# A new execution order and new buffer places for a fused window-attention and squared-ReLU kernel

## The chip, the core and the metric

The kernel runs on one core of a Trainium2 chip. The metric is the device time of one execution in microseconds (us); the figure is the median of repeated executions. The engines are PE (matrix products), ACT (activations), DVE (vector work), POOL and SP; POOL, SP and ACT also issue DMA transfers, each into a queue of its own that it works through in order.

## The reference

Sliding-window attention over 8 batches, 8 heads, 576 positions and a head width of 64, followed by a two-layer perceptron with a squared ReLU on the 4608 tokens.

```python
B, H, S, D = q.shape                      # 8, 8, 576, 64
scores = scale * np.matmul(q, k.transpose(0, 1, 3, 2))
mask = np.abs(pos[:, None] - pos[None, :]) <= 32
scores = np.where(mask, scores, -1000000000.0)
attn = softmax(scores)
x = np.matmul(attn, v)                    # heads side by side: 4608 x 512
h = x @ w_in                              # 512 x 2048
r = np.maximum(h, 0.0)
out = (r * r) @ w_out                     # 2048 x 512
```

Inputs and output are float32; inside, the kernel works in bfloat16 with float32 sums.

## The kernel before, in words

**Tiling.** The 576 positions of a batch are cut into three pieces of 192 queries, so there are 24 groups G = 0 to 23. POOL loads pieces of q, k and v from memory with a cast to bfloat16 (`load_qk`, L377; `load_v`, L415) into four `raw` buffers and five `v` buffers, and the weights (L431, L436). The first k and q pieces come through SP and ACT instead, uncast (`load_hw`, L391), and are cast on DVE (L394) and ACT (L393).

**Attention of a group.** q and k have to be turned so that the head width lies on partitions. For G below 9 PE does it (`turn_pe`, L463, with an evacuation at L476 or L477); from G = 9 on, a DMA that transposes does it, issued by SP (`turn_dma`, L491, names td<batch><piece><half>; it reads `raw` and writes `kq`). Then come the scores (L531, S<G>), the exponential on ACT (L554), the mask on DVE (L562), the product with v (L590, P<G>A and B), its normalisation on DVE into `xa` and `xb` (L604, L608), and the turning of the result into the ring `xt`: on PE for G below 9, by two transposing DMAs on SP from G = 9 on (`xturn`, L649 from `xa`, named T<G>a; L652 from `xb`, named T<G>b).

**The perceptron.** Tokens from 1536 on go through the first product in blocks of 512 by a fast scheme with 7 products in place of 8 (`mm1s`, L770, names Q<token>.<m><product>). It needs four sums of parts of `xt`, made on DVE (L742, xs0 to xs3 of a block), and the corrections c22 and c12 that DVE adds while it takes the products out of PSUM (L794). Earlier tokens take the plain product (L690). The second product is plain for the first 512 tokens (L835) and takes the 7-product scheme afterwards (`strassen`, L917, names P<block>.<product>), with sums on DVE (L885) and results evacuated on ACT (L670) or DVE (L949). 36 stores of 256 KB go out through ACT (L847) or SP (L848).

**What sets the order.** `record` lists 1480 operations in a fixed sequence, each with an engine, what it reads and writes, and, for some, a second form for another engine (`alt`). A planner that is not in the file has decided the rest, and its decision is the string `ORDER`: first one token for each recorded operation, a letter for the engine (P, A, D, G for POOL, S for SP) and the planner's due time in ns; then one token for each buffer that an operation uses (492 of them), its place in its pool. `apply` gives every operation its engine and place, and sorts all by due time; each engine gets its instructions in that order. Due times are not waited for: an instruction runs when its engine comes to it and the semaphores of what it depends on are there.

```python
for op in self.ops:
    s = next(order)
    op.start = int(s[1:])
    op.eng_ = ("PE", "ACT", "DVE", "POOL", "SP")["PADGS".index(s[0])]
...
self.out = sorted(self.ops, key=lambda o: (o.start, o.i))
```

`fill` then puts idle products of zeros (L299) into the gaps that the due times leave on PE at the start, 39 at least and one for each 56 ns of a gap, until the first operation that uses PSUM bank 7.

Of the kernel before, what the change touches and what calls it, by code (L numbers as in the profile page):

```python
# [2 lines left out]

ALU = mybir.AluOpType
# [52 lines left out]
    ALTB=300,  # L57
)
# [174 lines left out]
class Gen:  # L233
# [7 lines left out]
    def alloc(self):  # L241
# [155 lines left out]

    def vcopy(self, G):
        return G % 3 > 0 and G >= self.cfg["VC"]

    def load_v(self, b, g, key, after=None):
        G, NV = 3 * b + g, self.cfg["NV"]
        vt = self.V[G % NV]
        for j in range(2):
            k0 = 192 * g - 32 + 128 * j
            lo, hi = max(k0, 0), min(k0 + 128, S_)
            if self.vcopy(G) and j == 0:
                lo += 64
                vs, vf = self.V[(G - 1) % NV][64:128, 1, :, 0:64], vt[0:64, 0, :, 0:64]
                self.p.rec("DVE", lambda e, vs=vs, vf=vf: e.tensor_copy(vf, vs), reads=[("v", (G - 1) % NV, 1)], writes=[("vc", G % NV)],  # L410
# [4 lines left out]
            self.p.rec("POOL", lambda e, j=j, lo=lo, hi=hi, k0=k0: e.dma_start(  # L415
                vt[lo - k0:hi - k0, j, :, 0:64], self.v[b, :, lo:hi, :].rearrange("h p d -> p h d")),
                writes=[("v", G % NV, j)], dma=(f"v{G % NV}{j}", G), key=key, dur=500 + 3 * n, move=(n // 2, 13.5),
                name=f"v{b}{g}{j}", after=after, slack=self.cfg["LSLACK"] if b > 1 else 0)
# [27 lines left out]
    def turn_pe(self, t, b, g, key):  # L446
# [5 lines left out]
        pr = 3 * b + g < self.cfg["PR"]  # L452

        def f(e):
            ps = self.bank(v).bitcast(BF16)
            for j in range(4):
                for x in range(2):
# [5 lines left out]
                    mm = e.transpose(ps[:, n * j + h * x:n * j + h * x + h], at, self.ID[0:h, 0:h])  # L463
# [6 lines left out]
        def src():  # L470
            ps = self.bank(v).bitcast(BF16)[:, 0:4 * n]
            return ps.rearrange("p (j x q) -> p j q x", j=4, x=2) if pr else ps.rearrange("p (j q) -> p j q", j=4)

        if pr:
            dst = dst.rearrange("p j (q x) -> p j q x", x=2)
        fa = lambda e: e.activation(dst, src(), ACTF.Copy)  # L476
        fd = lambda e: e.tensor_copy(dst, src())  # L477
        if t == "q":
            self.p.rec("ACT", fa, reads=[v], writes=w, key=key, dur=act(4 * n), name=f"ev{t}{b}{g}",
                       alt=("DVE", dve(4 * n, not pr), fd) if self.cfg["ALT"] else None, bias=0)  # L480
        else:
            self.p.rec("DVE", fd, reads=[v], writes=w, key=key, dur=dve(4 * n, not pr), name=f"ev{t}{b}{g}",
# [84 lines left out]
    def pv(self, G):  # L567
# [10 lines left out]
        for w in range(2):  # L578
# [15 lines left out]
            rd = [("v", G % NV, w), ("vset", G % NV), pt] + ([("vc", G % NV)] if w == 0 and cfg["VC"] < NG else [])  # L594
# [138 lines left out]
    def mm1s(self, t0, key):  # L733
# [5 lines left out]
        b11, b12, b21, b22 = xt[:, 0:2, r:r + 256], xt[:, 0:2, r + 256:r + 512], xt[:, 2:4, r:r + 256], xt[:, 2:4, r + 256:r + 512]  # L739
        for i, a, b, rd in ((0, b12, b11, st[0] + st[1]), (1, b22, xs[0][:], st[1] + [("xs", 0)]),  # L740
                            (2, b22, b12, st[1]), (3, b21, xs[1][:], st[0] + [("xs", 1)])):
            p.rec("DVE", lambda e, o=xs[i][:], a=a, b=b: e.tensor_tensor(o, a, b, ALU.subtract), reads=rd, writes=[("xs", i)],  # L742
                  key=key, dur=dve(512), name=f"xs{i}.{t0}")
        tag = lambda f, h: [("gt", (t0 // 64 + 4 * h + x) % (GRING // 64), d) for x in range(4) for d in f]
        for m in range(4):
# [46 lines left out]
            def fused(src, tg, u, y, kk, nm, hh=hh, add=add):  # L792
                hs = lambda y=y: self.rt(hh)[:, 512 * y:512 * y + 512]
                add.append(p.rec("DVE", lambda e: e.tensor_tensor(hs(), src(), self.oe(u), ALU.add), reads=[tg, u],  # L794
                                 writes=[(hh, y)], key=kk, dur=dve(512, False), name=nm, uses=[v, hh], after=add[0] if y else None))
                if y or not cfg["FP"]:
# [3 lines left out]
                    p.rec("DVE", lambda e: e.tensor_scalar(src2(), src2(), 0.0, None, ALU.max), reads=rd, writes=rd, key=kk, dur=153 + 0.26 * c,  # L800
# [6 lines left out]

            prod(1, ks[0])
# [3 lines left out]
            one(X, xtag, rt, lo, ks[1], f"{t0}.{m}")  # L812
# [5 lines left out]
            fused(Y, ytag, p5, 0, ks[4], f"c22.{t0}.{m}")  # L818
            prod(3, ks[5])
            fused(X, xtag, u2, 1, ks[5], f"c12.{t0}.{m}")  # L820
            prod(4, ks[6])
            one(Y, ytag, rt2, hi, ks[6], f"{t0}.{m}b")
# [43 lines left out]
    def sums_g(self, g, key):  # L866
# [3 lines left out]
        for c in (0, 1, None):  # L870
            whole = c is None
            if whole and not cfg["S34"]:
# [353 lines left out]
```

## Time and profile before

| | |
|---|---|
| median of 3 runs (lowest to highest) | 286.65 us (286.6 to 287.02) |
| the profiled execution: its span | 287.0 us |
| PE busy | 279.1 us, 97% |
| DVE, ACT, POOL busy | 238.0, 215.7, 115.0 us |
| granted PE clock | 0.999 of full speed |
| loads through POOL's queue | 17.93 MB |
| transposes and stores through SP's queue | 15.34 MB |

The profile is of one execution. Its span runs from the first to the last instruction of the program, the wait for the last stores included; it lies 0.35 us above the median and within the highest run. A row of the timeline reads: start in us, duration in us, engine, line of the kernel, operation, what it writes and reads, how many instructions were merged, and in brackets the idle time of the engine before it with what ended it. PEld is PE's weight load, which is a separate row from the product. SPq and ACTq are DMA issues.

### The profile page before, as it was taken

What the parts mean: (1) busy time and instruction counts of PE and PEld (TensorE: products, weight loads), DVE (VectorE), ACT (ScalarE), POOL (GpSimd) and SP (SyncE); (2) the same over time, 40 slices, a digit from 0 to 9 for tenths busy, and PEclk for the clock granted to TensorE, in tenths of its full rate; (3) what the DMA queues carried; (4) which work ended last, traced back from release to release, by engine and by line L of the source; (5) the groups of instructions that cost most, each with busy time, mean ns of one, the idle gap of its engine ahead of it and who ended that gap; (6) DMA issues with size and microseconds to landing.
All of it is one profiled execution on the core that took longest, in us unless ns stands there. A gap on an engine that the chain in (4) does not pass through costs nothing.

```text
span 287.0 us, 7773 instructions
## 1 busy us (share of the span) xinstructions
PE 279.1 (97%) x3137; PEld 234.6 (82%) x3151; DVE 238.0 (83%) x438; ACT 215.7 (75%) x328; POOL 115.0 (40%) x153
## 2 busy tenths in 40 slices
PE   8999999999999999998999999999999999999995
PEld 8879866787756688886898888888888888888884
DVE  4787797989887798996899989998989978898721
ACT  2787666857868787887887889988887688798620
POOL 8999867194498052076235912605000000000000
PEclk9999999999999999999999999999999999999999
DMA  9999999999999999999999996989941612200233
GB/s 143 165 193 185 204 173 156 156 113 152 119 158 175 190 112 147 190 115 163 163 154 134 151 166 144 132 180 118 145 98 46 130 34 61 75 0 2 73 112 110
DMA packets 162915, 37.57 MB, mean 131 GB/s; under 512 B 150080, under 2 KB 162368, under 8 KB 162880
## 3 DMA queue, kind: packets, MB, share of 16 engines
q0 software_dynamic: 113728, 17.93, 87.7%
q1 hardware_dynamic: 44432, 15.34, 29.8%
q10 hardware_dynamic: 4720, 3.80, 5.1%
q8 instruction: 25, 0.41, 0.6%
q14 instruction: 10, 0.08, 0.1%
HBM read 36.70 MB, written 9.44 MB: 161 GB/s over the span
## 4 chain that ended last, share of the span: by engine, by line
PE 78%; DMA 10%; POOL 6%; DVE 2%; issue 2%; ACT 1%; ACTq 0%; DVEq 0%; POOLq 0%
PE ps L917 31%; PE ps L770 24%; PE ps L690 9%; PE ps L835 4%; POOL raw L377 4%; PE ps L590 3%; DMA w<-in_moe_w_in_dram 3%; PE ps L531 3%; DMA kq<-raw 3%; DMA v<-in_v_dram 2%; POOL v L415 2%; DMA xt<-xa 2%; PE ps L463 1%; DVE rt L794 1%; PE ps L630 0%
## 5 line engine op out<-in xcount | busy, mean ns | idle before, releaser
L665 ACT ACTIVATE rt<-ps 128x512 bf16<-128x512 f32 (+2 forms) x81 | 48.4, 606 | 17.6 <-PE ps L690 7.3
L670 ACT ACTIVATE oe<-ps 128x512 f32<-128x512 f32 x72 | 42.0, 595 | 22.2 <-PE ps L917 15.1
L554 ACT ACTIVATE e<-ps 128x1024 bf16<-128x1024 f32 x48 | 48.8, 1022 | 6.8 <-PE ps L531 5.0
L377 POOL DMA_DIRECT2D raw<-in_q_dram x46 | 36.7, 809 | 42.3 <-DMA kq<-raw 39.0
L377 POOL DMA_DIRECT2D raw<-in_k_dram x46 | 36.8, 816 | 27.2 <-DMA kq<-raw 20.8
L917 PE MATMUL ps<-w,gt 128*128 128x256 bf16 x384 | 47.0, 273 | 0.0
L690 PE MATMUL ps<-xt,w 128*128 128x192 bf16 (+2 forms) x379 | 46.4, 271 | 0.6 <-DMA w<-in_moe_w_in_dram 0.2
L415 POOL DMA_DIRECT2D v<-in_v_dram x48 | 38.6, 814 | 12.4 <-ACT v L412 10.0
L917 PEld LDWEIGHTS ps<-w,gt 128*128 128x128 bf16 x384 | 36.6, 98 | 4.9 <-issue 0.2
L770 PE MATMUL ps<-xs,sw 128*128 128x256 bf16 x288 | 39.9, 272 | 0.0
L690 PEld LDWEIGHTS ps<-xt,w 128*128 128x128 bf16 x384 | 32.4, 98 | 8.8 <-ACT v L412 0.3
L659 ACT ACTIVATE gt<-rt 128x512 bf16<-128x512 bf16 (+2 forms) x51 | 38.7, 777 | 0.3
L794 DVE TENSOR_TENSOR rt<-ps,oe 128x512 bf16<-128x512 f32 x48 | 32.9, 688 | 5.1 <-PE ps L770 3.8
L917 PE MATMUL ps<-ts,gt 128*128 128x256 bf16 x256 | 31.9, 273 | 0.0
L562 DVE TENSOR_TENSOR pt<-e,mask 128x2048 bf16<-128x2048 bf16 (+1 forms) x30 | 30.2, 1007 | 1.9 <-ACT e L554 1.4
L917 PE MATMUL ps<-ts,ss 128*128 128x256 bf16 x256 | 31.7, 273 | 0.0
L770 PEld LDWEIGHTS ps<-xs,sw 128*128 128x128 bf16 x288 | 27.4, 98 | 3.3 <-ACT oe L670 0.2
L770 PE MATMUL ps<-xt,w 128*128 128x256 bf16 x192 | 27.2, 273 | 0.2
L917 PEld LDWEIGHTS ps<-ts,ss 128*128 128x128 bf16 x256 | 24.7, 98 | 3.2
L660 DVE TENSOR_TENSOR gt<-rt 128x1024 bf16<-128x1024 bf16 (+2 forms) x49 | 26.4, 557 | 0.8 <-ACT rt L665 0.7
L917 PEld LDWEIGHTS ps<-ts,gt 128*128 128x128 bf16 x256 | 24.5, 98 | 3.2 <-DVE oe L949 0.3
L770 PEld LDWEIGHTS ps<-xt,w 128*128 128x128 bf16 x192 | 18.1, 98 | 3.3 <-ACT ps L809 0.4
(70 smaller groups left out, 405.2 us busy)
## 6 DMA issues: line engine op xcount, KB each, us to landing
out_dram<-oe SPq DMA_DIRECT2D x23, 256.0 KB, 3.5
out_dram<-oe ACTq DMA_DIRECT2D x13, 256.0 KB, 4.4
v<-in_v_dram POOLq DMA_DIRECT2D x16, 128.0 KB, 5.5
w<-in_moe_w_in_dram POOLq DMA_DIRECT2D x4, 512.0 KB, 9.8
w<-in_moe_w_out_dram POOLq DMA_DIRECT2D x4, 512.0 KB, 16.4
raw<-in_q_dram POOLq DMA_DIRECT2D x18, 96.0 KB, 5.3
raw<-in_k_dram POOLq DMA_DIRECT2D x14, 112.0 KB, 5.3
raw<-in_q_dram POOLq DMA_DIRECT2D x14, 112.0 KB, 6.9
```

The costliest lines, as they stand in the source:

```text
L377: self.p.rec("POOL", lambda e, j=j, dst=dst: e.dma_start(dst, s[j]), writes=[self.rtag(t, b, g, j)], dma=(f"{t}{G % self.cfg['NRAW']}{j}", ...
L415: self.p.rec("POOL", lambda e, j=j, lo=lo, hi=hi, k0=k0: e.dma_start(vt[lo - k0:hi - k0, j, :, 0:64], self.v[b, :, lo:hi, :].rearrange("h ...
L554: last = self.p.rec("ACT", lambda e, ef=ef, v=v: e.activation(ef(), self.bank(v, 0, 2), ACTF.Exp, scale=0.125), reads=[v], writes=tags, ke ...
L562: self.p.rec("DVE", lambda e, pf=pf, ef=ef, mb=mb, n=n: e.tensor_tensor(pf(y=0, n=n), ef(y=0, n=n).rearrange("p (w h q) -> p w h q", w=n, ...
L659: alt = ("ACT", act(c), lambda e: e.activation(dst, src(), ACTF.Square)) if self.cfg["ALT"] else None
L660: self.p.rec("DVE", lambda e: e.tensor_tensor(dst, src(), src(), ALU.mult), reads=rd, writes=wr, key=key, dur=dve(c), name=name, alt=alt, ...
L665: return self.p.rec("ACT", lambda e: e.activation(dst(), src(), ACTF.Relu), reads=rd, writes=wr, key=key, dur=act(c), name=name, alt=alt, ...
L670: self.p.rec("ACT", lambda e: e.activation(dst(), src(), ACTF.Copy), reads=rd, writes=wr, key=key, dur=act(c), name=name, alt=alt, bias=se ...
L690: mm = e.matmul(ht[:, n * x:n * x + n], self.W1[:, ft, 128 * d:128 * d + 128], self.XT[:, ft, r:r + n], start=(ft == 0 and x == 0), stop=( ...
L770: mm = e.matmul(bk[:, 256 * x:256 * x + 256], lhs(k, 256 * m + 128 * x), rhs[:, k, :], start=start and x == 0 and k == 0, stop=(k == 1), s ...
L794: add.append(p.rec("DVE", lambda e: e.tensor_tensor(hs(), src(), self.oe(u), ALU.add), reads=[tg, u], writes=[(hh, y)], key=kk, dur=dve(51 ...
L917: mm = e.matmul(op[:, 256 * y:256 * y + 256], lhs[:, l0[0] + k, a:a + 128], rhs[:, r0 + k, c0:c0 + 256], start=start and y == 0 and k == 0 ...
```

## The change

The configuration gets ten new switches, all off or at the value that leaves the code as it was (`AS=0, PS=0, VS=99, VD=0, ZP=0, XM=0, WIDE=(), JT=0, JM=0, SH=1`), with code behind them that is not reached (`vsplit`, `swapped`, `joint`, `wide`, `pair` and branches in `load_v`, `turn_pe`, `mm1s`, `strassen` and `sums_g`). One allocation is reached:

```diff
-            self.XS = [sb(f"xs{i}", [128, 2, 256], BF16) for i in range(4)]
+            self.XSA = sb("xs", [128, 4, 2, 256], BF16)
+            self.XS = [self.XSA[:, (0, 2, 1, 3)[i], :, :] for i in range(4)]
```

The four buffers become four parts of one, of the same size. What is left of the change is the string `ORDER`: the same number of tokens, with nearly all due times and many places new.

```diff
 ORDER = """
-D900 G1350 A1170 D2200 D5546 D9773 D10213 D10698 D7178 D9553 D11762 D7058 D7598 D10413 D11962 D9453 D5746 D17653 D5256
...
+D850 G2426 A1120 D3076 D3596 D5351 D6811 D10525 D2876 D6491 D9773 D5571 D11477 D4016 D6711 D3496 D1340 D18725 D4301
...
```

Counted token by token, 76 operations go from one of ACT and DVE to the other, 38 each way; 10 stores go from ACT to SP and 3 from SP to ACT, the last one of the program among the 10; no other operation changes its engine. Due times of the operations that the prediction speaks of, in ns (an operation's token is found by its place in the recorded sequence):

| operation | token | before | after |
|---|---|---|---|
| the iota that masks and identity need (POOL) | 2 | G1350 | G2426 |
| q001, the first load on POOL | 39 | G1700 | G850 |
| w11, second quarter of w_in (POOL) | 56 | G11936 | G11436 |
| turnk00, the first product that is not idle | 66 | P7128 | P7681 |
| A0.4, which needs w11 | 157 | P20637 | P20878 |
| T10b, then xs0.1536, which needs it | 526, 547 | S95574, D103850 | S96462, D100990 |
| td500, turning q and k of a later group (SP) | 824 | S110507 | S126368 |
| T13a, then xs0.2048, which needs it | 705, 707 | S122484, D130056 | S122088, D128824 |
| Q1536.33, Q1536.34 (PE) | 616, 620 | P131000, P131650 | P130303, P131614 |
| T15b, then xs2.2560, which needs it | 856, 881 | S149029, D156037 | S148009, D155940 |
| P8.4b, the last product | 1478 | P281083 | P280760 |
| the last store | 1480 | A282859 | S282535 |

On SP's queue the order around T13a becomes:

```
before: T10b T9b T10a td410 st6 td420 td500 T12a td421 T11b td501 T12b T11a T13a td510 td521
after:  T10a T10b td410 td411 td421 st2 td420 T11a T11b st6 st4 T12a T12b T13a td501 td521 st5 td500
```

POOL's 149 instructions keep their kind and number. By due time, 25 of its loads stand between 68 and 90 us (20 before), 20 between 101 and 117 us (7 before), 2 between 117 and 136 us (13 before), 22 between 136 and 154 us (10 before) and 10 from 154 us on (25 before). The idle products that `fill` makes from the due times become 159 in place of 149, and 78 of them stand ahead of turnk00 in place of 68.

More of the change, by code (lines that the diff above doesn't have):

```diff
@@ L57 @@
     ALTB=300,
+    AS=0,
+    PS=0,
+    VS=99,
+    VD=0,
+    ZP=0,
+    XM=0,
+    WIDE=(),
+    JT=0,
+    JM=0,
+    SH=1,
 )
@@ L452, in turn_pe @@
         pr = 3 * b + g < self.cfg["PR"]
+        il = pr and not self.cfg["PS"]
         def f(e):
@@ L811, in mm1s @@
             prod(2, ks[1])
[L812 removed]
+            if cfg["ZP"]:
+                pair(za, 0, X, xtag, None, ks[1], f"{t0}.{m}", ha)
+            else:
+                one(X, xtag, rt, lo, ks[1], f"{t0}.{m}")
             prod(6, ks[2])
@@ L871, in sums_g @@
             whole = c is None
-            if whole and not cfg["S34"]:
+            if whole and not cfg["S34"] or not whole and not cfg["SH"]:
                 continue
@@ L894, in wash @@
         if v.wash:
-            e.matmul(self.bank(v, 1), self.ZZ[:, 0:128], self.ZZ[:, 0:512], start=True, stop=True)
+            for i in range(v.n // 2, v.n):
+                e.matmul(self.bank(v, i), self.ZZ[:, 0:128], self.ZZ[:, 0:512], start=True, stop=True)
     def product(self, g, i, key, v):
```

414 lines of the change are left out of this document (293 added, 121 removed), and 10 rows, old and new, of the table ORDER.

## The prediction

> **What bounds the kernel now.** I read the page first, then the busy time by stages.
>
> ```profile
> span 287.0 us, 7773 instructions
> PE 279.1 (97%) x3137; PEld 234.6 (82%) x3151; DVE 238.0 (83%) x438; ACT 215.7 (75%) x328; POOL 115.0 (40%) x153
> ```
>
> ```profile
> core 0: us, PE busy (x) PEld busy (x) DVE busy (x) ACT busy (x) POOL busy (x), PEclk, DMA share, GB/s
> 1.00:21.00 20.00, 19.31 (x310) 17.39 (x311) 14.09 (x46) 12.52 (x18) 19.68 (x27) 1.00 1.69 174
> 21.00:126.00 105.00, 103.72 (x1200) 81.36 (x1213) 90.83 (x166) 79.89 (x115) 60.41 (x79) 1.00 1.72 157
> 126.00:134.00 8.00, 6.67 (x70) 5.30 (x69) 5.80 (x13) 5.48 (x9) 7.74 (x10) 1.00 2.20 154
> 134.00:283.62 149.62, 149.38 (x1562) 130.52 (x1562) 127.16 (x216) 116.90 (x187) 26.85 (x35) 1.00 0.81 106
> ```
>
> PE is the bound, and its real work is the same in both orders, so the change can only move PE's idle time, the idle products of the start, and the tail. PE is idle 1.28 us in the 105 us to 126, 0.24 us in the last 150 us, and 1.33 us in the 8 us between. That one spot is the largest thing an order could win. The timelines of DVE and of PE's weight loads show what happens there.
>
> ```profile
> 130.02 0.69 DVE L949 TENSOR_TENSOR oe<-ps,oe 128x512 f32<-128x512 f32 x1 [0.74 <-PE ps L917]
> 132.17 0.76 DVE L742 TENSOR_TENSOR xs<-xt 128x512 bf16<-128x512 bf16 x2 [1.46 <-DMA xt<-xa]
> 132.85 0.68 DVE L794 TENSOR_TENSOR rt<-ps,oe 128x512 bf16<-128x512 f32 x1
> 131.55 0.42 PEld L770 LDWEIGHTS ps<-xt,sw 128*128 128x128 bf16 x4
> 133.59 0.33 PEld L770 LDWEIGHTS ps<-xs,w 128*128 128x128 bf16 x4 [1.61 <-DVE rt L794]
> ```
>
> DVE stands 1.46 us in front of xs0.2048, which needs the transpose T13a. Queued behind it is the correction c22.1536.3 (L794, 132.85), and PE's Q1536.34 waits for that one before it may write the bank (133.59). The SP queue tells why the transpose was late.
>
> ```profile
> 116.05 1.22 SPq L491 DMA_TRANSPOSE kq<-raw  x1
> 117.32 1.24 SPq L649 DMA_TRANSPOSE xt<-xa  x1
> 118.66 1.23 SPq L491 DMA_TRANSPOSE kq<-raw  x1
> 119.93 2.19 SPq L652 DMA_TRANSPOSE xt<-xb  x1
> 122.23 1.24 SPq L491 DMA_TRANSPOSE kq<-raw  x1
> 123.51 1.27 SPq L652 DMA_TRANSPOSE xt<-xb  x1
> 124.83 2.58 SPq L649 DMA_TRANSPOSE xt<-xa  x2
> ```
>
> ```profile
> SPq L210 <- DMA raw<-in_q_dram: 11.4, 2, 6.0
> ```
>
> From 116.05 to 127.41 SP issues eight transposes without a pause, most of them 1.2 to 1.3 us. The first, td500, is due at 110.5 in the order and starts 5.5 us late, since SP waits in its queue for a load of q. T13a is the last of the eight: issued by about 126.1 (124.83 plus half of 2.58) against a due 122.5, and read by DVE at 132.17.
>
> ```profile
> 20.99 0.82 PE L690 MATMUL ps<-xt,w 128*128 128x192 bf16 x8 [0.17 <-DMA w<-in_moe_w_in_dram]
> 281.61 1.74 PEld L917 LDWEIGHTS ps<-ts,gt 128*128 128x128 bf16 x16
> ```
>
> The due times may be used as a ruler, not as a price, because PE follows them. A0.4 is due 20.64 and Q1536.33 131.00; they ran at 20.99 (first row here) and 131.55, lags of 0.35 and 0.55. Behind the stall Q1536.34 (due 131.65, ran 133.59) lags 1.94, and P8.4a (due 280.21, the second row) 1.40. So nothing behind the stall makes it good.
>
> **The change part by part.**
>
> *The stall at 132.* In the new SP order td500, td501 and td521 stand behind T13a, td421 stands far ahead, and T11a, T11b, T12a and T12b are spread over 15 us by due time. No load that can be late holds the queue just ahead of T13a. What its landing takes is bounded by the view of its line, min/median/max in the last row.
>
> ```profile
> L649 SPq DMA_TRANSPOSE xt<-xa x15: 1171/1242/2589, 92.8 to 238.6; - x15
> ...
> DMA to landing us min/median/max: 2.3/3.3/7.1
> ```
>
> By due times 6.74 us lie between its issue and its reader (122.09 to 128.82), double the median and 0.4 short of the worst; and only 2 loads are due from 117 to 136, so I take the median. The wait goes. What comes late next on DVE there is nothing: c22.2 (L949) moves behind xs0 and xs1, and its 0.74 us of waiting for PE is then covered. Worth: 1.33 us by PE's idle time, 1.61 by the weight load's; I take 1.33, since products drain while the weight load stands. At the worst landing, 7.1 us, 0.4 us of the wait come back.
>
> *The start.* PE stands on idle products until real work begins, and the fill is made from due times.
>
> ```profile
> 1.19 6.36 PE L299 MATMUL ps<-zz 128*128 128x128 bf16 x68 [1.19 <-DVE zz L293]
> 7.74 0.59 PEld L299 LDWEIGHTS ps<-zz 128*128 128x128 bf16 x10
> 0.83 0.23 POOL L307 IOTA dif<- 128x128 f32 x1 [0.39 <-POOLq L1211]
> 1.39 1.68 POOL L377 DMA_DIRECT2D raw<-in_q_dram  x2 [0.32 <-issue]
> ```
>
> Ten more idle products ahead of turnk00 cost 10 x 0.059 = 0.6 us there. Against that, the iota no longer stands in front of the first load, which starts 1.39 - 0.83 = 0.56 us earlier, and with it the whole queue of loads in front of w11, whose landing ended PE's last wait of the start (0.17 us ahead of A0.4). Between the two lie gaps that are filled with idle products, so most of the 0.6 is absorbed before 21 us. Bounds: -0.2 (w11's wait goes, the rest is absorbed) to +0.6 (all ten carried through). I take +0.1, nearer to the wait's row than to the fill's, as the wait is on the path and the fill is padding.
>
> *The swaps of engine.* Where a form has both engines in the trace:
>
> ```profile
> L670 ACT ACTIVATE oe<-ps 128x512 f32<-128x512 f32 x72 | 42.0, 595 | 22.2 <-PE ps L917 15.1 <-PE ps L770 4.8 <-PE ps L835 0.9
> L669 DVE COPY oe<-ps 128x512 f32<-128x512 f32 x12 | 8.3, 689 | 2.6 <-PE ps L770 1.3 <-PE ps L917 1.2
> L659 ACT ACTIVATE gt<-rt 128x512 bf16<-128x512 bf16 x30 | 18.3, 627 | 0.2
> L660 DVE TENSOR_TENSOR gt<-rt 128x512 bf16<-128x512 bf16 x18 | 7.2, 417 | 0.0
> 284.34 0.38 ACTq L847 DMA_DIRECT2D out_dram<-oe  x1
> ```
>
> 38 go each way, so the sums hardly move: an evacuation is 0.09 us dearer on DVE, a square 0.21 cheaper. ACT loses 7 stores net, 7 x 0.38 = 2.7 us, to SP. All of it lies under PE, which waits 0.24 us in the last 150 us with these engines 85% and 78% busy; cost 0. If that cover were gone, one swap in front of PE is worth about 0.1 to 0.2 us either way.
>
> *The remaining small waits of PE*, 1.28 us before 126 and 0.24 behind 134, belong to other pairs of neighbours in the new order. I take no change, 0.3 either way.
>
> *The tail.* The last store goes from ACT, whose issue took 0.38 us (the row above), to SP, behind a semaphore. No row shows that pair on SP; I bound it by 0 and by one such issue more, 0.4, and take 0, since it is one issue for one issue. Buffer places and the one xs allocation change no instruction: 0.
>
> *Loads in bursts.* This is what the change adds. Loads stand closer: 25, 20 and 22 in three stretches of some 20 us. The transposes run beside them, and the views of lines L652 and L491 give what that does.
>
> ```profile
> L652 SPq DMA_TRANSPOSE xt<-xb x15: 1190/1218/2193, 99.2 to 235.1; - x15
> ...
> DMA to landing us min/median/max: 2.4/4.0/6.5
> L491 SPq DMA_TRANSPOSE kq<-raw x30: 1203/1254/3492, 65.6 to 210.9; - x30
> ...
> DMA to landing us min/median/max: 2.7/4.4/7.9
> ```
>
> Two readers on DVE have a transpose close ahead: xs0.1536 behind T10b (96.46 to 100.99, 4.5 us, six transposes back to back) and xs2.2560 behind T15b (148.01 to 155.94, 7.9 us, inside the burst of 22). At the medians neither waits. At the worst, T10b's reader stands 6.5 - 4.5 = 2.0 us and T15b's 0. By due times no load is issued from 89.1 to 101.2, so I take the median for T10b: 0, with 2.0 kept for the range.
>
> The Trainium skill, "DMA: Bandwidth & Descriptors", section "Issuing engines are not separate DMA queues", speaks against the change here: transfers issued from SP and from POOL end on the same 16 engines and interleave, so a second queue gives no second road. The trace agrees in part: a transpose of one line took 2.7 us at best and 7.9 at worst. By the rule alone the bursts would slow the transposes, and the time would be that of the first or the third rival below.
>
> *Sum:* 287.0 - 1.33 + 0.1 = 285.8 for a profiled span; taken from the median, 286.65 - 1.23 = **285.4 us**. The profiled span lies 0.35 above the median, as one run in three did.
>
> **The rivals.**
>
> *The wait moves.* T10b lands 6.5 us after issue and DVE stands 2.0 us at xs0.1536; the correction c22.1 and PE's P1.4 are queued behind it. PE lost 1.33 of DVE's 1.46 in the old stall, so it loses about 1.9 here, less some 0.5 for the small waits that it has before 126 anyway: 286.65 - 1.23 + 1.4 = 286.8. For it: six transposes in a row, 1.25 us each. Against it: no load is due while the six are issued, and half of this line's transposes landed within 4.0.
>
> *It does not do what it says.* Due times are not waited for; POOL's early loads wait for their raw buffers, and SP for the loads, so the queues could run as before and T13a be late again: 286.65 or up to 0.3 less. Against it: the order in SP's queue itself has changed.
>
> *Slower, by the burst at 136 to 154.* Loads there are twice as dense (22 for 10). If what crowding adds to a transpose, 7.9 - 4.4 = 3.5 us, doubles, T15b lands 4.4 + 7.0 = 11.4 us after issue and DVE stands 3.5 us at xs2.2560, with c22.3 behind it and P3.4 waiting on that. By due times P3.4 stands 0.3 behind c22.3, so PE loses about 3.2: 286.65 - 1.23 + 3.2 = 288.6. It decides from a landing 10.0 us after issue (7.9, the 0.3, the gain of 1.23 and 0.57 more). For it: DMA share 2.20 in the crowded stretch of the table above. Against: no transpose took over 7.9.
>
> **How the numbers follow.** A measurement of this kernel can tell about 0.2%, 0.57 us, from no change. The forecast has 0.64, with its own range 284.8 (the start 0.2 shorter, 1.33 regained, 0.3 of small waits less: 286.65 - 1.83) to 286.0. The moved wait has 0.16 and the change that does nothing 0.06, both near 286.7; the burst has 0.14, from 287 up, as smaller overruns count to it. The range 284.9 to 287.0 leaves out most of the burst and a little at the low end. Faster by over 0.2% 0.64, within 0.22, slower 0.14.
>
> **What would show it.** Right: no DVE wait on xt over 0.3 us near 129, PE idle under 0.5 us between 126 and 134, SP's queue without a run of eight transposes ahead of T13a, A0.4 within 0.4 us of 21. Wrong: a DVE wait on xt near 101 or 156 with PE idle behind it; transposes of L652 over 8 us; A0.4 past 21.5; a second half in which PE idles more than 0.6 us.

## The result and the profile after

The kernel after takes **289.27 us** (median of 4 runs, 288.95 to 292.35) against 286.83 us (4 runs, 286.6 to 287.41): a ratio of 1.0101, 95% interval 1.0068 to 1.0134. Forecast were 285.4 us and a range up to 287.0. Eleven more runs of the same kernel, beside 34 of before, gave a median of 288.74 us (286.61 to 292.89) against 286.88 (286.4 to 288.29), ratio 1.0042 (1.0011 to 1.0072). The ratios leave out executions more than 1.5% above the fastest of their kernel, the medians do not, and with this kernel the difference matters.

The page of after, then its busy time by stages:

```profile
span 287.6 us, 7804 instructions
PE 279.8 (97%) x3161; PEld 236.0 (82%) x3161; DVE 237.1 (82%) x438; ACT 215.9 (75%) x328; POOL 114.7 (40%) x153
```

```profile
core 0: us, PE busy (x) PEld busy (x) DVE busy (x) ACT busy (x) POOL busy (x), PEclk, DMA share, GB/s
1.00:21.00 20.00, 19.16 (x309) 17.59 (x311) 14.52 (x47) 10.22 (x14) 19.62 (x27) 1.00 1.65 175
21.00:126.00 105.00, 104.06 (x1220) 81.64 (x1220) 89.52 (x164) 84.90 (x121) 69.44 (x90) 1.00 1.88 162
126.00:134.00 8.00, 6.22 (x68) 5.13 (x66) 5.34 (x10) 5.61 (x9) 0.82 (x1) 1.00 1.62 189
134.00:285.04 151.04, 150.31 (x1572) 131.67 (x1570) 127.53 (x220) 114.87 (x186) 24.61 (x32) 1.00 0.77 101
```

PE's work is the same, and its last product ends at 284.35, so that 0.69 us of the last row lie behind it. The hole is again between 126 and 134 us, 1.78 us now, but something else makes it. DVE's timeline of after, then PE's weight loads and SP's issues:

```profile
129.62 0.42 DVE L780 TENSOR_TENSOR xs<-xt 128x512 bf16<-128x512 bf16 x1 [0.24 <-PE ps L812]
130.08 0.42 DVE L780 TENSOR_TENSOR xs<-xt,xs 128x512 bf16<-128x512 bf16 x1
132.83 0.69 DVE L1139 TENSOR_TENSOR oe<-ps,oe 128x512 f32<-128x512 f32 x1 [2.32 <-DMA out_dram<-oe]
```

```profile
133.57 0.77 PEld L1107 LDWEIGHTS ps<-ts,gt 128*128 128x128 bf16 x8 [2.05 <-DVE oe L1139]
```

```profile
122.75 1.17 SPq L681 DMA_TRANSPOSE xt<-xa  x1
124.09 2.68 SPq L523 DMA_TRANSPOSE kq<-raw  x2
126.82 0.61 SPq L1036 DMA_DIRECT2D out_dram<-oe  x1
```

The wait for T13a is short in this execution: xs0.2048 runs at 129.62 after 0.24 us of waiting (before: 132.17 after 1.46). T13a landed at 129.44, 6.69 us after its issue, just in front of its reader. The add behind it, c22.2 (L1139), is what stands now. It writes an `oe` buffer, and its releaser is a *store* that still reads that buffer. The store is st5. Before, ACT issued it (due 112.55) and c22.2 had another place; now c22.2 has the place of st5's buffer, and st5 is due at 125.918 on SP, issued at 126.82 behind T13a and two more transposes, and landed 5.89 us later. PE's next products wait 2.05 us for c22.2.

What transposes took from issue to landing, in the views of their lines in after (L681 was L649, L684 was L652, L523 was L491):

```profile
L681 SPq DMA_TRANSPOSE xt<-xa x15: 1171/1190/3100, 90.1 to 233.7; - x15
...
DMA to landing us min/median/max: 2.3/4.6/10.8
L684 SPq DMA_TRANSPOSE xt<-xb x15: 1188/1245/1854, 95.6 to 235.8; - x15
...
DMA to landing us min/median/max: 2.5/4.2/8.9
L523 SPq DMA_TRANSPOSE kq<-raw x30: 1204/1274/2467, 60.6 to 187.7; - x30
...
DMA to landing us min/median/max: 2.7/5.3/9.9
```

At best they are as quick as before (2.3 to 2.7 us); the median of L649's line rises from 3.3 to 4.6 and its maximum from 7.1 to 10.8.

### The profile page after: what moved, and what is told of

Its sections match the earlier page's. It is cut to its first block, busy times and chain, and to the rows that moved or that the text cites. A ratio compares the mean times of both kernels' runs of the same rounds, so it can differ in the third digit from the quotient of the medians.

```text
span 287.6 us, 7804 instructions
## 1 busy us (share of the span) xinstructions
PE 279.8 (97%) x3161; PEld 236.0 (82%) x3161; DVE 237.1 (82%) x438; ACT 215.9 (75%) x328; POOL 114.7 (40%) x153
## 4 chain that ended last, share of the span: by engine, by line
PE 90%; DMA 4%; POOL 2%; DVE 2%; issue 1%; ACT 0%; POOLq 0%; DVEq 0%; ACTq 0%
PE ps L1107 34%; PE ps L812 25%; PE ps L722 15%; PE ps L1023 5%; PE ps L622 4%; PE ps L563 4%; POOL raw L389 2%; DMA out_dram<-oe 2%; DMA v<-in_v_dram 2%; PE ps L495 1%; PE ps L668 1%; PE ps L662 1%; DVE oe L1139 0%; PE ps L311 0%; DVE xa L640 0%
## 5 line engine op out<-in xcount | busy, mean ns | idle before, releaser
L702 ACT ACTIVATE oe<-ps 128x512 f32<-128x512 f32 x75 | 43.8, 595 | 19.4 <-PE ps L1107 14.0
L389 POOL DMA_DIRECT2D raw<-in_k_dram x46 | 36.1, 791 | 22.2 <-DMA kq<-raw 13.2
L691 ACT ACTIVATE gt<-rt 128x512 bf16<-128x512 bf16 (+2 forms) x51 | 40.2, 802 | 0.7 <-DVE rt L847 0.2
L812 PE MATMUL ps<-xs,sw 128*128 128x256 bf16 x288 | 39.2, 273 | 0.1
L692 DVE TENSOR_TENSOR gt<-rt 128x512 bf16<-128x512 bf16 (+2 forms) x49 | 25.7, 544 | 0.8 <-ACT rt L697 0.5
```

Of the source, the lines that this page charges most:

```text
L389: self.p.rec("POOL", lambda e, j=j, dst=dst: e.dma_start(dst, s[j]), writes=[self.rtag(t, b, g, j)], dma=(f"{t}{G % self.cfg['NRAW']}{j}", ...
L691: alt = ("ACT", act(c), lambda e: e.activation(dst, src(), ACTF.Square)) if self.cfg["ALT"] else None
L692: self.p.rec("DVE", lambda e: e.tensor_tensor(dst, src(), src(), ALU.mult), reads=rd, writes=wr, key=key, dur=dve(c), name=name, alt=alt, ...
L702: self.p.rec("ACT", lambda e: e.activation(dst(), src(), ACTF.Copy), reads=rd, writes=wr, key=key, dur=act(c), name=name, alt=alt, bias=se ...
L812: mm = e.matmul(bk[:, 256 * x:256 * x + 256], lhs(k, 256 * m + 128 * x), rhs[:, k, :], start=start and x == 0 and k == 0, stop=(k == 1), s ...
```

## The experiments

Four theories stood against each other. **First:** the late store and the place of c22.2's buffer. **Second:** the crowd of transfers, wherever it falls. **Third:** the start. **Fourth**, formed when a trace of a long execution was there: the order on DVE at 101 us. All kernels but two, in which loads are thinned, are edits of tokens in `ORDER`; a token is an engine letter and a due time, or a buffer's place. Kernels named together shared a chip and its runs of before.

### The stall that the forecast wanted to remove

**The kernel before, once more**, and **the kernel before with td500 moved** away from the front of SP's run of eight transposes:

```diff
-td500: S110507
+td500: S122600
```

Expected of the first:

> The kernel before, profiled once more, with nothing changed. If the wait of DVE on T13a near 132 us belongs to the kernel, this profile shows it again (1.3 to 1.6 us of PE idle between 126 and 134) and its time is that of the runs shown. If it belongs to one execution only, PE is idle under 0.4 us there, the span is about 285.5, and 1.3 us of the predicted gain never were to be had. It also shows how far the time lies above the span.

Expected of the second:

> The kernel before, with one token changed: the transpose td500 goes behind T13a in SP's queue (due 122.6 in place of 110.5), which is the one part of the new order that the prediction's gain rested on. By the prediction T13a is issued near 122.5, the wait of DVE near 132 goes, and the time falls by 1.0 to 1.4 us. If that wait does not stand in the usual executions of before, the time stays within 0.3 us.

Measured: 287.25 us, ratio 1.0008 (0.9991 to 1.0025), and 286.86 us, ratio 1.0009 (0.9993 to 1.0025). The stage from 126 to 134 us of the first:

```profile
126.00:134.00 8.00, 8.00 (x84) 6.69 (x83) 7.26 (x16) 6.72 (x12) 4.27 (x6) 1.00 2.18 172
```

PE never stops there, and it never stops there in the second kernel either (8.00 of 8). Five traces have SP's order ahead of T13a as it is in before, and two of them show the stall: the one that was shown before the prediction, and that of a kernel further down in which v000 comes late. Its row on DVE:

```profile
133.18 0.76 DVE L742 TENSOR_TENSOR xs<-xt 128x512 bf16<-128x512 bf16 x2 [1.36 <-DMA xt<-xa]
```

In these two SP issued td500 at 116.05 and 116.36, in the other three at 111.0 to 111.9. The kernel before, once more:

```profile
111.89 2.69 SPq L491 DMA_TRANSPOSE kq<-raw  x1
```

So the late td500 is there in some executions, and not in the usual one. The execution shown before the prediction was a long one: wherever a span and a run time stand side by side, the time is 1.8 to 2.2 us above the span (289.54 beside 287.6 in after, 287.36 beside 285.5 here), and 1.8 to 1.9 with the kernel before. Its span of 287.0 thus stands for about 288.8 us by this estimate (its own run time is not known), and 4 of 148 executions of before took that long. Nearly nothing of the gain was there to be had in the median.

### The late store

**The kernel after with store 5 early on ACT**, on two chips, and **with store 5 on ACT at its late time**:

```diff
-st5: S125918
+st5: A112650        (early, both chips)
+st5: A125918        (ACT, late)
```

Expected, early:

> The kernel after, with one token changed: the store st5 (result c12.1) is issued by ACT at its place of before (due 112.65) and not by SP at 125.92. Theory of the late store: c22.2 on DVE waits for the place in the oe pool that st5 still holds, so this wait (2.32 us on DVE, 2.05 on PE at 133.6) goes and the time falls by 1.7 to 2.1 us. Rival, crowded DMA queues: transposes and stores around 120 to 134 take 6 to 11 us whatever the store does, the next late one (T13a landed 0.2 us before its reader) takes the wait over, and the time falls by under 0.8 us.

Expected, early, beside the unaltered kernel after:

> The kernel after with store 5 alone issued by ACT at its former due time 112.65 (was SP, 125.918), beside the unaltered kernel after on the same chip. First theory (the late store holds the buffer that the add for group 2 needs): 0.6 to 1.0 % below the kernel after, that is within 0.4 % of the kernel before, and PE busy for all of 126 to 134 us. Second theory (the crowded DMA engines slow transposes and stores in many places): at most 0.3 % below the kernel after, and PE idle elsewhere between 95 and 160 us.

Expected of that unaltered kernel:

> The kernel after, unaltered, once more and on the same chip as the other three. Both theories: 0.7 to 1.3 % over the kernel before (288.8 to 290.6 us). If the late store (first theory) is what takes the time, the profiled execution shows PE idle for 1 to 2.5 us between 126 and 134 us again, with the vector add that writes the oe buffer waiting for a store's transfer; if that stall is absent in this execution, its time should be under 288 us.

Expected, ACT, late:

> The kernel after, with only the engine of st5 changed: ACT issues it, at the same due time of 125.92. If its landing is late because it stands behind the transposes in SP's queue, it lands within 4.4 us (median of ACT's stores before) of an issue near 126.5, c22.2 waits under 0.6 us, and the time falls by 1.4 us or more. If all 16 DMA engines are crowded whatever queue it is, it lands 5.5 to 6 us after issue again and the time falls by under 0.5 us.

Measured: early, 287.57 us, ratio 1.002 (0.999 to 1.005), and on the other chip 286.99 us, 1.0016 (0.9997 to 1.0034), where the unaltered kernel took 288.74 us, 1.0042. That is 0.26% by the ratios, less than the 0.6 to 1.0 that the first theory wanted, and their intervals overlap. The traced execution of the unaltered kernel there (287.61 us) lost only 0.4 us of PE in the stage, with the store landing 3.5 us after its issue. On ACT but late, 287.31 us, 1.0005 (0.9971 to 1.0038). With the store early the stage is full; the kernel of the second chip:

```profile
126.00:134.00 8.00, 8.00 (x86) 6.86 (x84) 7.17 (x14) 7.11 (x11) 1.01 (x1) 1.00 1.72 172
```

On ACT at the late time, the traced execution (span 287.2) still had PE busy 6.50 of these 8 us and DVE waiting 1.67 us for the store. ACT had issued it at 124.44, ahead of its due time and with no transpose in its queue, and it took 7.8 us to land:

```profile
out_dram<-oe ACTq DMA_DIRECT2D x1, 256.0 KB, 7.8
```

That execution was long (289.35 us), and the median and its wide interval do not show such a loss. How much of the hold is the place behind the transposes, and how much the flight of the store, the runs do not tell.

**The kernel before with this cost put in**: store 5 late on SP, c22.2 in its buffer, four other adds moved to make room.

```diff
-st5: A112550   c22.2/st11: place 4
+st5: S125918   c22.2/st11: place 2   (c22.1536.2: 2 to 1, c12.1536.3: 2 to 4, c22.2048.0 and .1: 2 to 4)
```

> The kernel before with the suspected cost put in and nothing else of the change: store 5 goes to SP with the due time 125.918 (was ACT, 112.55), and the add for group 2 (due 129.37) gets the buffer that this store holds; four other adds exchange buffers to make that room. First theory: the add waits until the store has landed (issued at 125.9 to 127, 3 to 6 us in flight, so 129 to 133 us) and the kernel is 0.2 to 1.0 % slower than before, with PE idle 0.5 to 2.5 us between 126 and 136 us. If the buffer and the queue of one store are worth nothing: within 0.2 % of before.

Measured: 287.66 us, ratio 1.0032 (1.0017 to 1.0048). DVE's row and PE's wait:

```profile
130.00 0.69 DVE L949 TENSOR_TENSOR oe<-ps,oe 128x512 f32<-128x512 f32 x1 [1.36 <-DMA out_dram<-oe]
```

```profile
PE ps L917 <- DVE oe L949: 0.7, 1, 0.7
```

In this execution the store was issued at 124.59, even ahead of its due time, and released its buffer at 130.00. The first theory holds: put in, the hold costs 0.32%, clear of noise, and taken out of after it gives back 0.26% of the ratio. It is not all, for the spread of after remained open.

### The crowd, first try

**The kernel after with eight loads thinned**: v511, v500, q600, q511, k601, k511, k600 and q601 (issued 110 to 117 us) move one head of eight.

```diff
+            src = s[j]
+            if f"{t}{b}{g}{j}" in THIN:
+                dst, src = dst[:, 0:1], src[:, 0:1]
```

> The kernel after, in which the eight last loads of the burst of 20 (v511, v500, q600, q511, k601, k511, k600, q601, issued from 110 to 117 us) move one head of eight only, so an eighth of their bytes; their other heads are left out of what is computed with. Store 5 stays on SP behind the transposes. Second theory (crowding): transposes and store 5 around 120 to 130 us land in 3 to 4.5 us instead of 6 to 7, and the time falls by 0.5 to 1.0 %, to within 0.4 % of before. First theory (the place in the queue): the store is still issued at 126 to 127 us and lands 3 to 4 us later, at 130 to 131, so 0.5 to 1.2 us of the wait of 2 to 2.8 stay and 0.4 to 0.8 % over before remain.

Measured: 286.87 us, ratio 0.9991 (0.9972 to 1.001). The store was issued at 127.67, later than in after, but T13a landed after 2.31 us (after: 6.69) and the store after 3.73 (after: 5.89), and PE was busy for all of 126 to 134. So the second theory has a share too: the hold bites because transfers around it are slow. At 5.89 us of flight this store would have landed at 133.56, 2 us behind the 131.52 at which c22.2 ran.

### The start

**v000 back ahead of k021, k020 and v010** in after; the same with store 5 early; and **v000 behind v010 in before**:

```diff
-v000: G8100   (after)        -v000: G7168   (before)
+v000: G5920                  +v000: G8710
```

Expected, after with v000 early:

> The kernel after with one load of the start, v000, back ahead of k021, k020 and v010 on POOL (due 5.92 instead of 8.10), where before had it nearer to; store 5 stays late. Third theory (the start: P0A, due 13.35, waits up to 1.2 us for v000, which lands at 12.7 to 13.9): the wait of the first values product for its load goes, PE is busy at least 19.5 of 20 us from 1 to 21, the time falls by 0.3 to 0.5 %, and the executions over 290.5 us (5 of 11 in the unaltered kernel after, at a mean granted clock of 0.988 to 0.994) become 0 or 1 of 12. First theory (store 5): ratio to before 1.003 to 1.011 as for after, and over 290.5 us in 2 to 5 of 12.

Expected, with store 5 early too:

> The kernel after with v000 early and store 5 early on ACT, both. First theory alone: as with store 5 early alone, ratio 1.001 to 1.003. Third theory added: 0.996 to 1.001, and no execution over 290.5 us (3 of 22 with store 5 early alone).

Expected, before with v000 late:

> The kernel before with v000 put behind v010 on POOL (due 8.71 instead of 7.17), its place in the kernel after. Third theory: P0A (due 12.45) waits 0.5 to 1.5 us for v000 (landing 13 to 13.7 instead of 11.9), and 0.1 to 0.5 % is lost, with executions over 290 us if the start is what makes them. First theory says nothing of it; if the wait at the start is made up for by idle time that the start has anyway (PE has gaps of 5 us in the plan's first 21 us): within 0.1 % of before.

Measured: 288.96 us, 1.0047 (1.0015 to 1.0079), nothing gained; with store 5 early 288.24 us, 1.0028 (0.9998 to 1.0058). In before the late v000 cost 0.72% (0.48 to 0.95): its traced execution shows PE waiting 0.9 us for v000, 0.6 us for a turned k or q, and 1.2 us behind T13a, in the stall of before (its row stands above). The 0.72%, 2.1 us, is more than the wait for v000; how often the other two waits come with it is left open. Four of its nine executions had a mean granted clock of 0.994, which none of 148 of before had, so a late start can bring on such executions. But it is not what brings them on in after, where they stay with v000 early (5 of 12): there the third theory falls.

The first of these kernels gave the trace that was missing, of an execution of 292.4 us. Its busy time by stages:

```profile
95.00:104.39 9.39, 9.23 (x104) 6.93 (x101) 4.72 (x8) 6.83 (x8) 3.14 (x4) 1.00 1.56 166
104.39:107.80 3.41, 0.97 (x13) 0.55 (x11) 2.82 (x7) 1.35 (x2) 1.58 (x3) 1.00 1.77 167
107.80:114.60 6.80, 5.53 (x37) 3.75 (x38) 5.45 (x8) 2.26 (x4) 6.80 (x10) 0.50 2.04 220
114.60:126.00 11.40, 11.40 (x118) 10.26 (x117) 9.26 (x17) 9.56 (x16) 3.96 (x5) 1.00 2.06 155
```

This is one execution, and among the longest. PE does 0.97 us of work in 3.41, and then its granted clock is 0.50 for 6.8 us: a product of 128x256 takes 419 ns in the mean there, and 273 in the unaltered kernel after. The groups of that stretch, and of 95 to 126 us in the unaltered kernel:

```profile
L1107 PE MATMUL ps<-ts,gt 128*128 128x256 bf16 x16 | 3.6, 419 | 1.5 <-DVE oe L1139 1.5
```

```profile
L1107 PE MATMUL ps<-ts,gt 128*128 128x256 bf16 x32 | 3.8, 273 | 1.1 <-DVE oe L1139 1.1
```

The timelines of DVE, ACT and PE's weight loads tell what stopped PE:

```profile
103.89 0.76 DVE L780 TENSOR_TENSOR xs<-xt 128x512 bf16<-128x512 bf16 x2 [4.45 <-DMA xt<-xb]
104.57 0.42 DVE L780 TENSOR_TENSOR xs<-xt,xs 128x512 bf16<-128x512 bf16 x1
105.02 0.21 DVE L636 RECIPROCAL rs<-ps 64x8 f32<-64x8 f32 x1
105.26 0.43 DVE L780 TENSOR_TENSOR xs<-xt,xs 128x512 bf16<-128x512 bf16 x1
105.72 0.69 DVE L640 TENSOR_TENSOR xa<-ps,rs 64x512 bf16<-64x512 f32 x1
```

```profile
106.45 0.60 ACT L646 ACTIVATE ps<-zz 64x520 f32<-64x520 bf16 x1 [3.42 <-DVE xa L640]
```

```profile
107.10 0.31 PEld L622 LDWEIGHTS ps<-v,pt 128*128 128x128 bf16 x8 [2.45 <-ACT ps L646]
```

DVE stands 4.45 us at xs0.1536 until T10b has landed, 5.86 us after its issue. Behind it in DVE's order is the normalisation of a group (L636, L640: R11A, N11A), ACT's next write to PSUM waits for that, and PE's next values product for ACT. The time from issue to landing of the last two loads of the burst (issued at 87.9 to 88.9 us), in this execution and then in one of the unaltered kernel after:

```profile
raw<-in_k_dram POOLq DMA_DIRECT2D x1, 112.0 KB, 13.5
raw<-in_q_dram POOLq DMA_DIRECT2D x1, 112.0 KB, 14.4
```

```profile
raw<-in_k_dram POOLq DMA_DIRECT2D x1, 112.0 KB, 6.3
raw<-in_q_dram POOLq DMA_DIRECT2D x1, 112.0 KB, 6.5
```

In the long execution the burst, whose last load was issued by 89.5 us, took twice as long, and its end was in flight beside T10b (issued at 97.91) until 103; in the other it had landed by 95.4.

The flight is not all of it. In the unaltered kernel T10b landed 2.5 us after its issue, and the add waited 1.48 us all the same:

```profile
98.49 1.27 SPq L684 DMA_TRANSPOSE xt<-xb  x1
```

```profile
101.11 0.76 DVE L780 TENSOR_TENSOR xs<-xt 128x512 bf16<-128x512 bf16 x2 [1.48 <-DMA xt<-xb]
```

SP had issued T10b 2.0 us behind its due time, and DVE was free 1.4 us ahead of that of the add. Of the 4.5 us that the due times leave between the two, 1.1 were left here, and 1.5 in the long execution.

### DVE's order at 101 us

The four adds that make xs for tile 1536 are due from 100.99 in after, ahead of R11A, N11A and c22.1; in before they stand at 103.85 to 105.18, behind all three. **Moved by little**, with v000 and store 5 early; **moved to just ahead of c22.1**, alone, with store 5 early, and with v000 early too; **moved behind c22.1**, with both:

```diff
-xs0.1536: D100990  xs2.1536: D101409  xs1.1536: D101828  xs3.1536: D102447
+all four: D102860 to D102866     (moved by little)
+all four: D104985 to D104988     (just ahead of c22.1)
+all four: D104995 to D104998     (behind c22.1)
```

Expected, moved by little:

> As the one before, and the four adds that make xs for tile 1536 go 0.4 to 1.9 us later on VectorE, behind R11A and N11A, so that the wait for transpose T10b (0.5 to 1.5 us at 101 us) finds less to hold up. If that wait reaches PE's products of group 1 at 106 us (0.8 to 1.5 us there): 0.1 to 0.4 % below the kernel with the two edits, ratio 0.994 to 0.999. If it is hidden: the same as that kernel within 0.1 %.

Expected, ahead of c22.1, alone:

> The kernel after; on VectorE alone the four adds that make xs for tile 1536 go behind R11A, N11A, the gate product g1024.14 and the sum s12.1 (due 104.985 to 104.988 instead of 100.99 to 102.45), just ahead of the add c22.1. Store 5 stays late. Fourth theory (VectorE's order at 101 us: the adds wait for transpose T10b, and the normalisation R11A and N11A, on which PE's next values products hang, stands behind them; PE idles up to 3.7 us and the gate halves its clock): executions over 290.5 us go from 5 of 11 to at most 1 of 12, PE is busy at least 30.3 of 31 us from 95 to 126; the stall at 133 stays, 287.5 to 289 us. Second theory (the crowd of transfers, whatever the order): executions over 290.5 us stay at 3 or more of 12.

Expected, with store 5 early:

> The same and store 5 early on ACT. First and fourth theory together account for the loss: ratio to before 0.996 to 1.001 by all its executions' median too (286.0 to 287.1 us), none over 290.5 us. If something else of the change costs as well: 287.3 us or more, or executions over 290.5 us.

Expected, with v000 early too:

> The same and v000 early at the start. Its place was worth 0 in the kernel after by the last runs (1.0047 beside 1.0042) and 0.7 % in the kernel before: expected equal to the kernel before it within 0.1 %, at best 0.3 % below.

Expected, behind c22.1:

> The kernel after with store 5 early on ACT, v000 early, and the four adds for xs of tile 1536 behind the add c22.1 (due 104.995 to 104.998; before has them behind c22.1 too), so that neither R11A and N11A nor c22.1 stands behind transpose T10b. First and fourth theory: no execution over 290.5 us, PE busy at least 30.5 of 31 us from 95 to 126, 286.0 to 287.0 us, ratio 0.996 to 1.000: the loss is gone, and it would be the fastest of the kernels with the new order. If the new order costs something else: 287.2 us or more with both stretches busy.

And **the kernel before with the order put in**, the four adds ahead of c22.1:

```diff
-xs0.1536: D103850  xs1.1536: D104340  xs2.1536: D104759  xs3.1536: D105178
+all four: D102620 to D102623     (c22.1 is due at 103.165)
```

> The kernel before with the suspected order put in: the four adds for xs of tile 1536 ahead of the add c22.1 on VectorE (due 102.62 instead of 103.85 to 105.18, c22.1 103.165), the transposes and loads as they are. Fourth theory: c22.1 waits behind the transposes of T10 (T10a was issued at 102.2 us and the adds ran at 104.7), so it runs at 106 to 107 instead of 103.8, PE waits 0.5 to 2 us for it at 105 to 107 us, and the kernel is 0.2 to 0.7 % slower. If VectorE's order is not what makes PE late: within 0.1 % of before.

Measured, with the number of executions whose mean granted clock was 0.994 or less:

| kernel | adds at | store 5 | median us | ratio (95%) | clock 0.994 or less |
|---|---|---|---|---|---|
| after, both times | 100.99 | late | 289.27, 288.74 | 1.0101, 1.0042 | 6 of 15 |
| v000 early | 100.99 | late | 288.96 | 1.0047 (1.0015 to 1.0079) | 5 of 12 |
| store early, both chips | 100.99 | early | 287.57, 286.99 | 1.002, 1.0016 | 3 of 22 |
| v000, store early | 100.99 | early | 288.24 | 1.0028 (0.9998 to 1.0058) | 4 of 12 |
| moved by little | 102.86 | early | 288.05 | 1.0046 (1.0013 to 1.0078) | 3 of 12 |
| ahead of c22.1 | 104.985 | late | 288.17 | 1.0053 (1.0025 to 1.008) | 2 of 12 |
| the same | 104.985 | early | 287.69 | 1.003 (1.0009 to 1.005) | 0 of 12 |
| the same, v000 early | 104.985 | early | 287.53 | 1.0024 (1.0009 to 1.0039) | 0 of 12 |
| behind c22.1 | 104.995 | early | 287.50 | 1.0034 (1.0018 to 1.0051) | 0 of 9 |
| before, beside these | 103.85 | as before | 286.69 to 287.0 | 1 | 0 of 148 |
| before, order put in | 102.62 | as before | 288.11 | 1.0052 (1.0039 to 1.0065) | 0 of 6 |

With the adds just ahead of c22.1 or behind it and the store early, none of 33 executions ran at such a clock; with both as in after, 11 of 27 did. Moved with the store late, the adds left 2 of 12, between what the fourth theory wanted (at most 1) and what the second did (3 or more); moved by little, some 2 us in front of c22.1, they left 3 of 12. Put into before, the order costs 0.52%, by the mechanism expected; DVE's rows and PE's wait in that kernel:

```profile
104.24 0.42 DVE L742 TENSOR_TENSOR xs<-xt 128x512 bf16<-128x512 bf16 x1 [1.47 <-DMA xt<-xa]
...
105.71 0.68 DVE L949 TENSOR_TENSOR oe<-ps,oe 128x512 f32<-128x512 f32 x1
```

```profile
PE ps L917 <- DVE oe L949: 1.5, 1, 1.5
```

The fourth theory holds for the executions at a low clock, but the expected 286.0 to 287.1 us was missed by every version with the adds moved, and so was the expected PE time of 30.3 us or more. The adds are needed soon after 107 us, and between normalisation and c22.1 they push other work: from 95 to 126 us PE is busy 29.89 of 31 us with the adds ahead of c22.1 and store 5 early (first row), against 30.71 where the adds stay put and T10b happens to be quick (second row).

```profile
95.00:126.00 31.00, 29.89 (x330) 25.01 (x329) 27.09 (x48) 23.82 (x34) 16.39 (x21) 1.00 1.55 165
```

```profile
95.00:126.00 31.00, 30.71 (x337) 25.77 (x336) 28.12 (x49) 24.02 (x35) 16.35 (x21) 1.00 1.51 156
```

So no place tried for the adds is good: early, they may stand behind the transpose; late, they cost 0.7 to 0.8 us against the second row in all four traced executions (29.89 to 30.00). Against before this is not clearly a loss: its two traces have 30.58 and 29.81 in this stretch.

Part of what these kernels lose lies outside the span. Run time less span is 1.76 to 1.89 us in all 148 executions of before, 1.89 to 2.07 in after and the other kernels with its order and store 5 on SP, and 2.10 to 2.23 in every kernel with store 5 on ACT. With the adds ahead of c22.1 and the store early, 0.8 us are lost by the medians of the time (287.69 beside 286.89) and 0.4 by those of the span (285.5 beside 285.1). What the part outside the span is, no run shows.

### The crowd, second try

**The kernel after with store 5 early and nine loads of the burst at 80 to 89 us thinned** (k411, v400, k420, q421, k421, q420, v411, k500, q501), DVE's order left as in after:

> The kernel after with store 5 early, in which nine loads of the burst at 80 to 89 us (k411, v400, k420, q421, k421, q420, v411, k500, q501) move one head of eight only; the other heads are left out of what is computed with. VectorE's order at 101 us is that of after. Second theory: T9b, T10a and T10b land in 2.3 to 4.5 us in every execution, the adds no longer wait, no execution over 290.5 us (3 of 22 before the thinning), 286.0 to 286.8 us. If the late transposes have another cause than this burst: as with store 5 early alone, 287.0 to 287.6 us with some over 290.5 us.

Measured: 287.20 us, ratio 1.001 (0.9991 to 1.0029), 0 of 12 at a clock of 0.994 or less. In its traced execution T9b, T10a and T10b landed after 2.52, 3.66 and 3.22 us (7.62, 6.67 and 5.86 in the long one), and PE was busy 30.88 us:

```profile
95.00:126.00 31.00, 30.88 (x341) 25.82 (x339) 28.88 (x50) 24.24 (x35) 16.42 (x21) 1.00 1.56 156
```

The expected 286.0 to 286.8 us was missed, but by the spans nothing is lost (medians of 285.0 beside 285.1): the 0.3 us lie outside. With these loads out of the way the order costs next to nothing; with the loads in place, no place tried for the adds was free. So by these runs it takes both, though the evidence on the loads is thin: T10b took 2.5 us in one execution with all loads too, and 0 of 12 is not far from 3 of 22. No kernel with the new order that computes everything was faster than before.

## Why the prediction was wrong

- **The stall at 132 (-1.33 us): two steps failed.** The first is the last step of the sum, which took a stall of one execution off the median, on the ground that "The profiled span lies 0.35 above the median". The run time lies about 1.8 us above the span, so that execution was some 2 us above the median, and the stall was most of that. In the usual execution of before PE does not stop there, and the kernel with td500 moved, which is this part of the change alone, gained nothing (1.0009). The second is "I take the median" for T13a: 3.3 us was taken for its landing, and it took 5.5 to 8.2 us in eleven traced executions of the new order with all loads in place and PE's clock at 1.00. That its reader waited only 0.24 us in the first of them, as forecast, was luck, for 6.69 us of flight met 6.74 of slack. In the execution with v000 and store 5 early it took 8.2, the add ran 0.2 us after it had landed (the profile names PE), and PE lost 0.9 us behind it:

```profile
xt<-xa SPq DMA_TRANSPOSE x1, 8.2
```

```profile
130.56 0.43 DVE L780 TENSOR_TENSOR xs<-xt 128x512 bf16<-128x512 bf16 x1 [1.75 <-PE ps L563]
```

- **"What comes late next on DVE there is nothing"** and **"Buffer places and the one xs allocation change no instruction: 0"** failed together. c22.2 was next, and late by its place: 2.05 us in the trace of after, 0.26 and 0.32% by the two experiments. A place changes no instruction but adds a wait for whoever held it last.
- **"All of it lies under PE ... cost 0" for the stores that go from ACT to SP** failed for one of ten. Its price was not the issue (0.61 us), but that it was 13 us later, with an add waiting for its buffer. On ACT, at the same late time, the ratio was 1.0005 (0.9971 to 1.0038), though its traced execution still had the wait.
- **The bursts: "By due times no load is issued from 89.1 to 101.2, so I take the median for T10b: 0."** The issues were counted, not the landings: in the long execution loads issued by 89.5 us were in flight up to 14.4 us, beside T10b. And the due times, "a ruler" for PE, were none for SP and DVE: the slack of 4.5 us was 1.1 to 1.5. The reader of T10b, kept for the range at 2.0 us, stood 1.5 us in one execution and 4.45 in another, and PE's clock made it worse.
- **The rivals.** "The wait moves" named this very place, with c22.1 behind it, and gave it 286.8 us; it left out the normalisation in the same queue and the clock. "Slower, by the burst at 136 to 154" had the right sign in the wrong place: xs2.2560 did not wait, and PE lost 0.05 us from 134 us to its last product at 284.35. T15b took 7.5 us, within the 7.9 that by due times it had.
- **The start (+0.1)** came out at both ends. A0.4 ran at 21.62 in after's first traced execution, 0.63 later than in before and past the 21.5 that was to show it wrong, and at 20.75 in the second, 0.24 earlier; these two rows:

```profile
21.62 0.82 PE L722 MATMUL ps<-xt,w 128*128 128x192 bf16 x8
```

```profile
20.75 0.83 PE L722 MATMUL ps<-xt,w 128*128 128x192 bf16 x8
```

  In the first, PE waited 0.5 us for a load of v, v000, that the forecast did not look at.
- **What held.** The small waits from 21 to 126 came to 0.94 us in after's traced execution, forecast 1.28 with 0.3 either way, and that is in part luck: in the stage's row of before, PE has 1200 products beside 1213 weight loads, so some 13 products are missing from the profile, each a hole of about 0.05 us that is no wait. In after's row none is missing (1220 and 1220). The rule of the Trainium skill, "DMA: Bandwidth & Descriptors", section "Issuing engines are not separate DMA queues", that was weighed against the change was the one to follow: by the two thinned kernels, what POOL loads sets how long a transfer from SP takes.

How the 1.86 us between the medians of 288.74 and 286.88 divide is not settled: store 5 is worth 1.75 of them by medians there (288.74 to 286.99) and 0.5 and 0.7 in the other two pairs, so part of it comes and goes with the number of long executions. By the ratios the hold is 0.19 to 0.26% in all three pairs, none of them clear of noise by itself. What makes the same loads land in 6.3 us in one execution and 13.5 in another was not found.

## What to carry to other kernels

Before a stall is taken off a median, see whether the median has it: compare the profiled execution's own run time, not its span, with the other runs, and profile the kernel once more. When an order or a buffer plan changes, follow each buffer to the transfer that still reads it and each in-order queue to what stands behind the instruction that waits; a store without a reader can hold up a product. Count transfers as in flight until they land, and leave slack in front of a reader by their worst landing, since a plan that is tighter by 3.7 us (8.3 to 4.5 by due times, from T10b to its reader) is paid for in some executions and not in others.

## What the runs showed of the hardware

- After a stretch of 3.41 us in which PE worked 0.97 us, the granted clock was 0.50 for 6.8 us. PE was busy for 5.53 of them, so by an estimate its work there took about 2.8 us longer than at full clock. A stall of 2.05 us in after's execution had no such end (clock 1.00 in all stages). The Trainium skill, "TensorE: Matmul & The Clock Gate", section "What's actually happening", has the clock halved after one idle window of about 3.4 us. The trace does not test the length, since the stretch was cut to it; it does show that the stretch need not be idle throughout, for this one was 28% busy.
- The same transpose (T10b) took 2.5 us in one execution and 5.86 in another at nearly the same issue time (98.49 and 97.91).
